# Attention and mixture of experts on one core: loads, casts and bindings moved around the change of phase

## The chip, the cores and the metric

The kernel runs on one core of a Trainium2 chip. The core has five engines with an instruction queue each: TensorE (PE in the profile, its weight loads PEld), VectorE (DVE), ScalarE (ACT), GpSimd (POOL) and SyncE (SP). SyncE computes nothing; it issues most of the DMAs. An engine takes its instructions in the order in which they were built, and one that waits holds up all that stand behind it. The metric is the device time of one execution in microseconds (us); lower is better.

## The reference

```python
def _attn_ref(q, k, v):                    # 8 batches, 8 heads, 576 positions, 64 wide
    ...
    out_d = sm_attn(q_d, k_d, v_d)         # on means of four positions
    out_up = np.repeat(out_d, factor, axis=2)
    ...
    scores = np.where(mask, scores, -1000000000.0)   # mask: |i - j| < 4
    ...
    return out_up + out_local

def _moe_ref(x, modality_id, w_gate, modality_bias, w1, w2):   # x: 4608 tokens, 512 wide
    logits = x @ w_gate + modality_bias[modality_id]
    e_idx = np.argmax(logits, axis=1)
    ...
    for e in range(E):                     # 8 experts, 512 -> 1024 -> 512
        mask = e_idx == e
        ...
        h = np.maximum(x[mask] @ w1[e], 0.0)
        out[mask] = gate_w[mask, None] * (h @ w2[e])
```

Attention over all batches gives the tokens; each token is then sent to one expert of eight.

## The kernel before

**Attention** runs in 32 stages of two heads (number n; batch b has n = 4b to 4b+3). The work of a stage is cut into steps, and the table PHASE gives each step a place after its stage's start, in stages. build() makes a list of calls (place, function), sorts it, and so writes the order of all engines by hand (tc.manual_schedule). A step of stage n with phase p has the place n + p. Steps that matter here: tp (transposes of q and k), sc and scd (scores; scd needs qd, which GpSimd sums from qe), le, exp, z, zr (softmax; z and zr on VectorE), nl (GpSimd scales the local weights with zr; on the profile's L426, tile le), nd (the same for tile de, L430), lt and Pw (turned weights), vp and vd (sums of v over four positions: a matmul on tile vw, L279, and its copy on VectorE, L284), avl (local output, L481), X (the sum of both, L488).

**Loads.** load_v(b, part) loads half of a batch's v into tile vw in four to seven DMAs (L266, L267). Two buffers vw take turns, so v of batch 7 overwrites that of batch 5. load_qk loads q and k of four heads (L244). store() writes finished tokens to the DRAM tensor xs (L634). SyncE has eight DMAs in flight at most: each waits, besides its own conditions, for the landing of the one eight ahead of it.

**Routing.** After each batch the router finds the expert and place of every token and GpSimd scatters token numbers and gates into the DRAM table tab (L640). The **early units** are two units of 512 tokens of one expert, taken from the first four batches, so that their work can begin where attention ends. moe.entries reads a unit's part of tab into a tile tg (L892). rows(u, h) then has GpSimd gather 128 of its tokens from xs into xg by those numbers (L935); the first gather of the first unit is placed at 28.64, just ahead of qe of stage 28. wload loads a 128x1024 block of the expert's first layer (tile raw, four DMAs, L849), wsplit casts it to a high part (GpSimd for the first four, L874) and takes the low part (VectorE, L880). Each product of the experts is three matmuls: high by high, high by low, low by high.

**Experts.** After the two early units (Moe.compute, first layer L1003, second layer Moe.second, L1057) come three large units of 1024 tokens (class Large), then small ones of 256, one of 128 (compute_half, H = 1, second to last) and one of 256. While early unit 1 computes, the first large unit is prepared by Large.put: "1W", "2W" cast its weights, "r0" to "r7" turn its rows, "S1", "T1" and the like are sums. In this part no order is written by hand, a scheduler sets it, and `tc.issue_after(ins)` binds what is traced inside it behind `ins` on that engine.

Of the kernel before, what the change touches and what calls it, by code (L numbers as in the profile page):

```python
# [11 lines left out]
AF = mybir.ActivationFunctionType  # L12
# [7 lines left out]
B, H, S, D = 8, 8, 576, 64  # L20
# [56 lines left out]
def whole(pieces):  # L77

    while True:
        try:  # L80
            next(pieces)
        except StopIteration as x:
            return x.value
# [720 lines left out]
class Moe:  # L804
# [180 lines left out]
    def compute(s, T, W, X, H=2, step=None, mid=None, J=None, last=0):  # L985
        nc = s.nc
        xh, xl = X
        hh, hl = s.hidden(H)
        N = 128 * H
        n = 4 // H  # L990
        early = H == 4 and s.turn["h"] == 0
        ps = {}
        for f, ks in [(f + j, k) for f in range(0, 8, 2) for k in ((0, 1), (2, 3)) for j in range(2)] if early else [
                (f, range(4)) for f in range(8)]:
            if step and f % 2 == 0 and 0 in ks:
                step()
            if f % n == 0 and 0 in ks:
                ps[f // n] = s.ps.tile([128, n, N], F32, name="l1", tag="S", bufs=SB)
            p, fs = ps[f // n], slice(128 * f, 128 * f + 128)
            for k in ks:  # L1000
                wh, wl = W[k]
                for i, (a, x) in enumerate(((wh, xh), (wh, xl), (wl, xh))):
                    nc.tensor.matmul(p[:, f % n, :], a[:, fs], x[:, k, :N], start=(k == 0 and i == 0),  # L1003
                                     stop=(k == 3 and i == 2))
            if f % n == n - 1 and 3 in ks:
                g = slice((f + 1 - n) % 4, f % 4 + 1)
                y, z = hh[f // 4][:, g, :N], hl[f // 4][:, g, :N]
                nc.scalar.activation(y, p, AF.Relu)  # L1008
                s.low = nc.vector.scalar_tensor_tensor(z, p, 0.0, y.bitcast(F32), op0=ALU.max, op1=ALU.subtract)  # L1009
        s.second(T, W[4:], hh, hl, H, step, mid, J, last)  # L1010

# [25 lines left out]
    def second(s, T, W, hh, hl, H, step, mid, J=None, last=0, large=False):  # L1037

        nc = s.nc
        if last:  # L1040
            with s.tc.issue_after(getattr(s.sent, "ins", s.sent)):
                nc.gpsimd.drain()  # L1042
        for h in range(H):
            if mid:
                mid(h)
            a, b, hs = (hh[h // 4], hl[h // 4], h % 4) if large else (hh, hl, h)
            hs = slice(128 * hs, 128 * hs + 128)

            first = large or s.turn["h"] == 0
            p = s.ps.tile([128, DM], F32, name="l2", tag="S" if first else "A", bufs=SB if first else 2)  # L1050
            for f in range(8):
                if step and f % (2 * H) == 0:
                    step()
                wh, wl = W[f // 2]
                y, z = a[f // 4][:, f % 4, hs], b[f // 4][:, f % 4, hs]
                for i, (l, x) in enumerate(((y, wh), (z, wh), (y, wl))):
                    nc.tensor.matmul(p, l, x[:, f % 2, :], start=(f == 0 and i == 0), stop=(f == 7 and i == 2))  # L1057
            o = s.xp.tile([128, DM], F32, name="o", bufs=3)
            nc.scalar.mul(o, p, T[:, h, 1:2].bitcast(F32))  # L1059
            if J is not None and not last and h < J.shape[1]:  # L1060
                o2 = s.out.rearrange("n (c d) -> (n c) d", c=2)
                for c in range(2):
                    s.sent = nc.gpsimd.indirect_dma_start(  # L1063
                        out=o2, out_offset=bass.IndirectOffsetOnAxis(ap=J[:, h, c : c + 1], axis=0),
                        in_=o[:, 256 * c : 256 * c + 256], in_offset=None, bounds_check=2 * NTOK - 1, oob_is_err=False)
                continue
            nc.gpsimd.indirect_dma_start(  # L1067
                out=s.out[:, :],
                out_offset=bass.IndirectOffsetOnAxis(ap=T[:, h, 0:1], axis=0),
                in_=o, in_offset=None, bounds_check=NTOK - 1, oob_is_err=False)  # L1070
# [123 lines left out]


def build(tc, q, k, v, mid, w_gate, bias, w1, w2, out):
    nc = tc.nc
    with ExitStack() as ctx:
# [6 lines left out]
        start = ExitStack()  # L1205
        start.enter_context(tc.manual_schedule())
        C = Consts(tc, cp, ps)
        moe = Moe(tc, ctx, C, ps, xs, tab, w1, w2, out)
        with ExitStack() as actx:
# [10 lines left out]
            C.clear(nc, cp)  # L1220
            at.load_v(0, 0)
            C.load(tc, cp, work, at.wk, mid, bias, w_gate)
            at.load_v(0, 4)
            at.load_qk(1, 0)
            start.close()
            ro.rp, ro.block = at.wk, moe.block
            N = 4 * B
# [15 lines left out]
            def call(at, f, *args):  # L1243
                calls.append((at, len(calls), f, args))

            P = PHASE
            parts = {"kT": "kT_", "Pw": "Pw_", "W": "store"}
# [5 lines left out]
            for nm, p in P.items():  # L1253
                f, i = (nm[:-1], int(nm[-1])) if nm[-1].isdigit() and nm not in ("ch1", "ch2") else (nm, 0)
# [6 lines left out]
            for b in range(B):  # L1261
                if b + 1 < B:
                    for j in range(2):
                        late_ = (1.39, 0.78)[j] if b == B - 2 else 0
                        call(4 * b - 1 + used + 0.3 + 0.8 * j - late_, at.load_v, b + 1, 4 * j)
            for h in range(3, N // 2):
                call(2 * h - 5 + last + 0.25, at.load_qk, h // 2, h % 2)
# [35 lines left out]
            def split(u):  # L1303
                piece(("x", u), lambda: moe.xsplit(E[u][2], 4), E[u].append)
# [21 lines left out]
            for u in range(KEARLY):  # L1326
                call(t + 1 + 0.1 * u, expert, u)
            for u in range(KEARLY):
                call(4 * (B - 2) + 1.3 + 0.01 * u, entries, u)
            for i, x in enumerate((0.64, 1.64, 2.64, 2.66)):  # L1330
                call(4 * (B - 1) + x, rows, 0, i)
            free = N - 1 + max(P["scd"], P["sc0"], P["sc1"]) + 0.02

            for c, x in enumerate((0.2, 2.4, 3.4, 4.4)):
                call(4 * (B - 2) + x, wload, c)
            for c in range(2):
                for j in range(2):
                    call(N - 1 + (0.15, 0.66)[c] + 0.25 * j, wsplit, c)
            calls.sort(key=lambda x: x[:2])
            with tc.manual_schedule():  # L1340
                for x in calls:
# [52 lines left out]
        lists, Es, Ts, Rs, Xs, parts = {}, {}, {}, {}, {}, {}  # L1394

        N, written = len(order), ExitStack()
# [3 lines left out]
        def gather(i):  # L1400
            nm, u, H = order[i]
            idx, ei = lists[nm]
            Es[i] = moe.expert(ei, u)
            if H == 8:
                x = Xs[i] = Large(moe, Es[i], u)
                if not u:
                    x.put("l0 l1")
                Ts[i] = x.T = moe.entries(idx, u, H)
                if u:
                    Rs[i] = [moe.unit_rows() for _ in range(2)]  # L1410
                else:
                    Rs[i] = [moe.gather(Ts[i][:, 4 * l : 4 * l + 4], H=4) for l in range(2)]
                x.R = Rs[i]
                return
            Ts[i] = moe.entries(idx, u, H)
            if i in cols:
                Js[i] = moe.columns(Ts[i], cols[i][0], cols[i][1])
            Rs[i] = moe.gather(Ts[i], H=H, J=Js.get(i))
# [37 lines left out]
        first = ("1W", "2W", "S1", "", "l2")  # L1456
        begin = ("r0 r1 r2 r3 5W S2", "r4 r5 r6 r7 1X 2X 6W", "T1 5X T2", "6X s4 t4")
# [4 lines left out]
        for i, (_, u, H) in enumerate(order):  # L1462
# [12 lines left out]
            if i < KEARLY:  # L1475
                turn = [0]

                def early_step():
                    if i == 1:
                        Xs[2].put(first[turn[0]] if turn[0] < len(first) else "")  # L1480
                    elif 0 < turn[0] < 6:
                        b, t = ((B - 2, 0), (B - 2, 1), (B - 1, 0), (B - 1, 1), (B - 1, 2))[turn[0] - 1]
                        with tc.issue_after(moe.low.ins):
                            for j in range(2):
                                ro.R(b, 2 * t + j)
                        ro.store(b, t)
                    turn[0] += 1

                def mid(h):
                    if i == 0:  # L1490
                        split(1, h)
                        if h == 3:
                            gather(2)
                    else:
                        Xs[2].put(begin[h])
                        if h == 1:
                            Js[3] = moe.pieces(lists["q"][0], 1)
                        elif h == 2:
                            moe.numbers(Js[3])

                moe.compute(Ts[i], Ws[i], Xs[i], H, early_step, mid)
            elif H == 8:
                q, count = Xs[i], iter(range(32))
# [62 lines left out]
        with tc.For_i(0, nu, 1) as iv:  # L1566
# [6 lines left out]
            Xs = whole(moe.xsplit(R))  # L1573
# [32 lines left out]
```

## Time and profile before

| what | value |
|---|---|
| time, median of 3 runs | 655.95 us (651.89 to 656.73) |
| the profiled execution's own time | 658.49 us |
| its span, first to last instruction | 656.4 us |
| PE busy / matmul instructions | 628.5 us / 6099 |
| DVE, ACT, POOL busy | 438.6, 383.9, 338.5 us |
| mean granted clock of TensorE | 0.988 |

The trace has two parts: attention up to about 242 us, then the experts. The profiled execution is one execution; it lies 2.5 us above the median of the others, and 2.1 us of its time lie outside the span.

### The profile page before, as it was taken

The page shows a single profiled execution, that of the slowest core. Times are in us where ns is not written, and L with a number is a line of the kernel's source. Part 1 is how long each engine was busy: PE and PEld are TensorE (multiplying, and loading weights), DVE is VectorE, ACT ScalarE, POOL GpSimd, SP SyncE. Part 2 cuts the span into 40 slices and gives each one's busy share as a digit, 9 for nine tenths or more (in the row PEclk, how much of TensorE's full clock was granted, in tenths as well). Part 3 has the DMA queues.
Part 4 walks back from the last instruction along what each step waited for, and adds up shares of the span by engine and source line. Part 5 has one row for each costly group of instructions (what it writes and reads, how often), then busy time and mean ns, then how long its engine had stood idle before and what let it go on. Part 6 is the DMA issues. An engine that isn't in the chain of part 4 may idle for free. (4 is left out here: it accounts for less than half of the span.)

```text
span 656.4 us, 16392 instructions
## 1 busy us (share of the span) xinstructions
PE 628.5 (96%) x6099; PEld 496.8 (76%) x6099; DVE 438.6 (67%) x896; ACT 383.9 (58%) x870; POOL 338.5 (52%) x378
## 2 busy tenths in 40 slices
PE   9899999999999789999999999999999999999995
PEld 5677677766777567887888788887888878889794
DVE  6689898899988865843455764777638875246610
ACT  4689999988999862312544732447324474245610
POOL 6644564745557761326069775688755720141211
PEclk9899999998999989999999999999999999999999
DMA  8899699999899975499012445134531345459300
GB/s 190 178 189 187 112 201 186 172 201 160 173 169 151 187 200 144 78 176 234 1 49 97 108 118 144 49 97 109 124 137 49 96 117 158 144 152 285 130 15 32
DMA packets 168860, 90.21 MB, mean 137 GB/s; under 512 B 131812, under 2 KB 153354, under 8 KB 168778
## 3 DMA queue, kind: packets, MB, share of 16 engines
q1 hardware_dynamic: 160810, 69.96, 51.2%
q0 software_dynamic: 7968, 19.18, 9.4%
q8 instruction: 49, 0.80, 0.6%
q14 instruction: 33, 0.27, 0.2%
HBM read 69.86 MB, written 19.51 MB: 136 GB/s over the span
## 5 line engine op out<-in xcount | busy, mean ns | idle before, releaser
L1057 PE MATMUL l<-V,H 128*128 128x512 f32 x792 | 183.7, 390 | 0.0
L1057 PEld LDWEIGHTS l<-V,H 128*128 128x128 f32 x792 | 148.0, 188 | 30.6
L943 POOL DMA_INDIRECT xg<-xs,m x64 | 74.4, 1163 | 19.2 <-issue 19.2
L426 POOL TENSOR_TENSOR le<-le,zr 128x384 f32<-128x384 f32 x32 | 26.6, 832 | 81.3 <-DVE zr L422 40.7
L1067 POOL DMA_INDIRECT out_dram<-o,tq x24 | 27.9, 1161 | 76.3 <-ACT o L1059 58.5
L442 ACT COPY Pw<-lt 32x288 f32<-32x288 f32 x128 | 54.6, 427 | 1.7
L1003 PE MATMUL l<-X,H 128*128 128x512 f32 (+1 forms) x240 | 53.9, 374 | 1.5 <-ACT X L979 1.0
L1059 ACT ACTIVATE o<-l,tq 128x512 f32<-128x512 f32 x24 | 16.6, 690 | 66.2 <-PE l L1057 41.4
L640 POOL DMA_INDIRECT tab<-ig,si x36 | 36.4, 1010 | 29.8 <-DVE mni L662 21.8
L1003 PEld LDWEIGHTS l<-X,H 128*128 128x128 f32 x240 | 41.5, 189 | 9.9 <-ACT X L979 1.3
L1160 ACT ACTIVATE H<-o 128x512 fp32r<-128x512 f32 x36 | 22.8, 634 | 39.2 <-DVE o L1182 39.2
L331 ACT COPY kT<-tp 64x512 f32<-64x512 f32 x64 | 37.2, 580 | 8.8 <-PE tp L294 7.3
L481 PEld LDWEIGHTS avl<-Pw,vw 128*64 128x64 f32 x768 | 33.6, 139 | 11.1 <-ACT kT L329 4.9
L880 DVE TENSOR_TENSOR V<-raw,V 128x1024 fp32r<-128x1024 f32 x22 | 35.1, 1621 | 9.9 <-ACT V L874 9.7
L481 PE MATMUL avl<-Pw,vw 128*64 128x96 f32 x768 | 39.7, 254 | 2.1 <-ACT Pw L442 2.1
L1009 DVE SCALAR_TENSOR_TENSOR H<-l,H 128x512 fp32r<-128x512 f32 x24 | 16.2, 687 | 34.5 <-ACT H L1008 34.4
L1067 POOL DMA_INDIRECT out_dram<-o,tg x10 | 11.3, 1129 | 51.6 <-ACT o L1059 35.5
L412 ACT ACTIVATE de<-scd,dm 128x144 f32<-128x144 f32 x96 | 35.2, 374 | 1.7 <-DVE dm L404 0.6
L373 PE MATMUL sc<-kT,qT 128*24 128x64 f32 x1536 | 34.8, 225 | 0.3 <-ACT qT L318 0.3
L1008 ACT ACTIVATE H<-l 128x512 fp32r<-128x512 f32 x24 | 13.9, 596 | 35.7 <-PE l L1003 35.7
L373 PEld LDWEIGHTS sc<-kT,qT 128*24 128x24 f32 x1536 | 24.6, 104 | 13.2 <-issue 10.8
L1121 DVE TENSOR_TENSOR G<-X,G 128x1024 fp32r<-128x1024 f32 x15 | 23.2, 1551 | 13.8 <-ACT G L1120 13.8
(282 smaller groups left out, 1435.5 us busy)
## 6 DMA issues: line engine op xcount, KB each, us to landing
raw<-in_moe_w_dram SPq DMA_DIRECT2D x112, 128.0 KB
raw<-in_moe_w_dram SPq DMA_DIRECT2D x28, 512.0 KB
vw<-in_v_dram SPq DMA_DIRECT2D x60, 180.0 KB
qt<-in_q_dram SPq DMA_DIRECT2D x26, 288.0 KB
kt<-in_k_dram SPq DMA_DIRECT2D x26, 288.0 KB
xs<-R SPq DMA_DIRECT2D x48, 128.0 KB
xs<-G SPq DMA_DIRECT2D x16, 128.0 KB
qt<-in_q_dram SPq DMA_DIRECT2D x6, 256.0 KB
```

The source lines that it names most:

```text
L331: s.nc.scalar.copy(s.kB[r, g, a, PAD + 64 * g : PAD + 64 * g + 512], p[r])
L373: s.nc.tensor.matmul(p[32 * j : 32 * j + SUB, 2 * i : 2 * i + 2, :], qT[:, q0 : q0 + SUB], kB[:, :, q0 : q0 + WIN], start=False, stop=(i = ...
L412: s.nc.scalar.activation(x, s.t["scd", n][:, c].rearrange("p (k x) -> p k x", k=NB), AF.Exp, bias=m[:, c : c + 1], accum_out=s.t["z", n][: ...
L426: s.nc.gpsimd.tensor_tensor(e, e, z[:, : 2 * NB].unsqueeze(2).broadcast_to([128, 2 * NB, WIN]), op=ALU.mult)
L442: s.nc.scalar.copy(s.Pw[n % NPW][r, :, j, :SUB], s.t["lt", n][r, :, :SUB])
L481: s.nc.tensor.matmul(p[64 * a : 64 * a + 64, c], vw[:, NB * (4 * (hp // 2) + hp % 2 + 2 * a) + k, :], Pw[:, 2 * k + a], start=True, stop=T ...
L640: i = nc.gpsimd.indirect_dma_start(out=s.tab[:, :], out_offset=bass.IndirectOffsetOnAxis(ap=C.si[:, t : t + 1], axis=0), in_=C.ig[:, t, :] ...
L880: (nc.gpsimd if turn == 4 else nc.vector).tensor_tensor(lo, raw, hi.bitcast(F32), op=ALU.subtract)
L943: s.nc.gpsimd.indirect_dma_start(out=R[l].rearrange("p h (i x) -> p (h i) x", i=4)[:, i, :], out_offset=None, in_=s.xs.rearrange("n (a x) ...
L1003: nc.tensor.matmul(p[:, f % n, :], a[:, fs], x[:, k, :N], start=(k == 0 and i == 0), stop=(k == 3 and i == 2))
L1057: nc.tensor.matmul(p, l, x[:, f % 2, :], start=(f == 0 and i == 0), stop=(f == 7 and i == 2))
L1067: nc.gpsimd.indirect_dma_start(out=s.out[:, :], out_offset=bass.IndirectOffsetOnAxis(ap=T[:, h, 0:1], axis=0), in_=o, in_offset=None, boun ...
```

## The change

Six things are changed. (1) Both halves of the last v (load_v for batch 7) get earlier places: 24.65 instead of 25.45 and 26.58 instead of 26.86. (2) The reading of the early units' entries goes from 25.30 to 26.62. (3) The first two weight blocks are loaded at 26.64 and 26.90 instead of 24.2 and 26.4, and their casts stand at 31.70 and 31.95 instead of 31.15 and 31.66. (4) The first puts of the large unit (1W, 2W, S1, l2) are bound behind the last ReLU of the early unit's first layer that has been traced. (5) The puts in its second layer are bound behind the last matmul of the first layer. (6) In the second layer of the unit with H = 1, four hidden blocks at a time take both products with the high part first and then the one with the low part.

```diff
-                    nc.tensor.matmul(p[:, f % n, :], a[:, fs], x[:, k, :N], start=(k == 0 and i == 0),
-                                     stop=(k == 3 and i == 2))
+                    s.mm = nc.tensor.matmul(p[:, f % n, :], a[:, fs], x[:, k, :N], start=(k == 0 and i == 0),
+                                            stop=(k == 3 and i == 2))
...
-                nc.scalar.activation(y, p, AF.Relu)
+                s.relu = nc.scalar.activation(y, p, AF.Relu)
...
-            for f in range(8):
-                if step and f % (2 * H) == 0:
+            for f, parts in [(f + j, x) for f in range(0, 8, 4) for x in ((0, 2), (1,)) for j in range(4)] if H == 1 else [
+                    (f, (0, 1, 2)) for f in range(8)]:
+                if step and f % (2 * H) == 0 and 0 in parts:
                     step()
                 wh, wl = W[f // 2]
                 y, z = a[f // 4][:, f % 4, hs], b[f // 4][:, f % 4, hs]
-                for i, (l, x) in enumerate(((y, wh), (z, wh), (y, wl))):
-                    nc.tensor.matmul(p, l, x[:, f % 2, :], start=(f == 0 and i == 0), stop=(f == 7 and i == 2))
+                for i in parts:
+                    l, x = ((y, wh), (z, wh), (y, wl))[i]
+                    nc.tensor.matmul(p, l, x[:, f % 2, :], start=(f == 0 and i == 0), stop=(f == 7 and i == (1 if H == 1 else 2)))
...
-                        late_ = (1.39, 0.78)[j] if b == B - 2 else 0
+                        late_ = (2.19, 1.06)[j] if b == B - 2 else 0
                         call(4 * b - 1 + used + 0.3 + 0.8 * j - late_, at.load_v, b + 1, 4 * j)
...
-                call(4 * (B - 2) + 1.3 + 0.01 * u, entries, u)
+                call(4 * (B - 2) + 2.62 + 0.01 * u, entries, u)
...
-            for c, x in enumerate((0.2, 2.4, 3.4, 4.4)):
+            for c, x in enumerate((2.64, 2.9, 3.4, 4.4)):
                 call(4 * (B - 2) + x, wload, c)
             for c in range(2):
                 for j in range(2):
-                    call(N - 1 + (0.15, 0.66)[c] + 0.25 * j, wsplit, c)
+                    call(N - 1 + (0.7, 0.95)[c] + 0.25 * j, wsplit, c)
...
                     if i == 1:
-                        Xs[2].put(first[turn[0]] if turn[0] < len(first) else "")
+                        with tc.issue_after(moe.relu.ins):
+                            Xs[2].put(first[turn[0]] if turn[0] < len(first) else "")
...
-                        Xs[2].put(begin[h])
+                        with tc.issue_after(moe.mm.ins):
+                            Xs[2].put(begin[h])
```

On SyncE before, around stage 25: the last block DMA of the first weights, the entries of both early units (tiles tg; ebi and eb hold their addresses), the last q and k, and the first half of the last v.

```order
L849 DMA raw_3700<-in_moe_w_dram 32x1024
L888 TENSOR_LOAD ebi
L888 ISA x2
L892 ISA
L892 DMA tg_3862<-tab 128x4x2
L888 TENSOR_LOAD eb_3338
L888 ISA x2
L892 ISA
L892 DMA tg_3874<-tab 128x4x2
L244 DMA qt<-in_q_dram 128x9x64 x2
L244 DMA kt<-in_k_dram 128x9x64 x2
L267 DMA vw_155<-in_v_dram 30x24x64 x4
```

The same place in the changed kernel; the first half of v (vw_155, x4) and qt x2 stand right ahead of these rows, and the first weights right behind the second tg.

```order
L244 DMA kt<-in_k_dram 128x9x64 x2
L267 DMA vw_155<-in_v_dram 30x24x64
L266 DMA vw_155<-in_v_dram 30x64
L267 DMA vw_155<-in_v_dram 30x23x64
L266 DMA vw_155<-in_v_dram 30x64
L267 DMA vw_155<-in_v_dram 30x23x64
L266 DMA vw_155<-in_v_dram 27x64
L267 DMA vw_155<-in_v_dram 30x23x64
L888 TENSOR_LOAD ebi
L888 ISA x2
L892 ISA
L892 DMA tg_4059<-tab 128x4x2
```

The entries stood behind four DMAs of weights; now fifteen DMAs of v, q and k stand between the same store of tokens and them.

On GpSimd before, from the last gather of the first early unit on: the two casts of weights (H_4733, H_4807), nl and nd (le, de), qe and qd of the last stage.

```order
L935 DMA xg<-xs,tg_3862 128x512
L874 CAST H_4733<-raw_3700 128x1024
L426 TENSOR_TENSOR le<-le,zr 128x384
L430 TENSOR_TENSOR de_168<-de_168,zr 128x18x24
L351 TENSOR_TENSOR qe<-qT 128x288
L355 TENSOR_TENSOR qd<-qe 128x144
L874 CAST H_4807<-raw_3700 128x1024
L1239 COPY X<-X 128x4x64
L426 TENSOR_TENSOR le<-le,zr 128x384
```

The same place in the changed kernel (the casts are H_4809 and H_4834).

```order
L935 DMA xg<-xs,tg_4059 128x512
L426 TENSOR_TENSOR le<-le,zr 128x384
L430 TENSOR_TENSOR de_168<-de_168,zr 128x18x24
L351 TENSOR_TENSOR qe<-qT 128x288
L355 TENSOR_TENSOR qd<-qe 128x144
L1241 COPY X<-X 128x4x64
L874 CAST H_4809<-raw_4072 128x1024
L874 CAST H_4834<-raw_4072 128x1024
L426 TENSOR_TENSOR le<-le,zr 128x384
```

Both casts now stand together, behind qd of the last stage and ahead of nl of stage 30. The gathers themselves keep their places on GpSimd.

On VectorE in the changed kernel, the low parts of the same two blocks (H_4809, H_4834) among the last stages' softmax steps; before, the first stood between lm and le of stage 30 and the second between its z and its zr.

```order
L416 TENSOR_REDUCE z<-le 128x4x3
L880 TENSOR_TENSOR H_4809<-raw_4072,H_4809 128x1024
L421 TENSOR_SCALAR zr<-z 128x15
L422 RECIPROCAL zr<-zr 128x15
L880 TENSOR_TENSOR H_4834<-raw_4072,H_4834 128x1024
L380 TENSOR_REDUCE lm<-sc 128x12
L437 STREAM_TRANSPOSE lt<-le 128x384
L404 TENSOR_REDUCE dm<-scd 128x3
L284 COPY vd<-vp 96x512
L488 TENSOR_TENSOR X<-avl,Od 128x288 x2
L385 TENSOR_TENSOR le<-sc,lm 128x384
L416 TENSOR_REDUCE z<-le 128x4x3
```

The low parts moved from the middle of stage 30's softmax to between its z and stage 31's lm.

## Rows read from the trace of the kernel before

**Rows 1.** Busy time of each engine by stretch: PE, PEld, DVE, ACT, POOL, clock, DMA share, GB/s

```profile
200.00:250.00 50.00, 42.03 (x657) 30.79 (x653) 35.45 (x73) 36.29 (x103) 37.69 (x40) 0.93 0.91 200
...
204.00:225.50 21.50, 18.64 (x389) 14.00 (x387) 17.20 (x39) 18.26 (x54) 20.00 (x24) 1.00 0.97 167
...
230.00:235.00 5.00, 5.00 (x52) 3.62 (x47) 2.44 (x6) 1.11 (x6) 0.00 (x0) 0.50 0.96 228
```

**Rows 2.** Timeline of PE, end of attention: start, us, line, tiles, [idle before <-releaser]

```profile
206.18 0.95 PE L399 MATMUL scd<-kd,qd 64*64 64x144 f32 x12 [0.65 <-POOL qd L355]
...
215.67 1.06 PE L279 MATMUL vp<-vw,pool 128*32 128x256 f32 x12 [1.42 <-DMA vw<-in_v_dram]
...
229.47 1.93 PE L279 MATMUL vp<-vw,pool 128*32 128x256 f32 x12 [2.40 <-DMA vw<-in_v_dram]
...
241.79 0.97 PE L1003 MATMUL l<-X,H 128*128 128x512 f32 x3 [0.99 <-ACT X L979]
```

**Rows 3.** Timeline of SyncE's DMA issues; us is issuing time, not landing

```profile
142.49 2.56 SPq L267 DMA_DIRECT2D vw<-in_v_dram  x4
...
153.77 4.83 SPq L267 DMA_DIRECT2D vw<-in_v_dram  x4
...
172.26 3.72 SPq L267 DMA_DIRECT2D vw<-in_v_dram  x4
...
184.35 4.40 SPq L267 DMA_DIRECT2D vw<-in_v_dram  x4
...
193.46 1.89 SPq L849 DMA_DIRECT2D raw<-in_moe_w_dram  x4
196.23 1.59 SPq L892 DMA_DIRECT2D tg<-tab  x2
...
201.82 5.91 SPq L267 DMA_DIRECT2D vw<-in_v_dram  x4
...
217.63 0.35 SPq L266 DMA_DIRECT2D vw<-in_v_dram  x1
...
293.61 0.40 SPq L892 DMA_DIRECT2D tq<-tab  x1
```

**Rows 4.** Timeline of POOL

```profile
203.87 1.05 POOL L935 DMA_INDIRECT xg<-xs,tg  x1 [0.30 <-issue]
...
205.70 0.43 POOL L355 TENSOR_TENSOR qd<-qe 128x144 f32<-128x144 f32 x1
...
219.21 1.04 POOL L874 CAST H<-raw 128x1024 fp32r<-128x1024 f32 x1
...
224.95 0.40 POOL L1239 COPY X<-X 128x256 f32<-128x256 f32 x1
227.27 0.83 POOL L426 TENSOR_TENSOR le<-le,zr 128x384 f32<-128x384 f32 x1 [1.92 <-DVE zr L422]
...
235.19 0.83 POOL L426 TENSOR_TENSOR le<-le,zr 128x384 f32<-128x384 f32 x1 [6.21 <-ACT PdT L459]
...
298.58 1.21 POOL L935 DMA_INDIRECT xg<-xs,tq  x1 [0.96 <-DMA tq<-tab]
```

**Rows 5.** Timeline of DVE, end of attention

```profile
221.45 1.55 DVE L880 TENSOR_TENSOR H<-raw,H 128x1024 fp32r<-128x1024 f32 x1
...
225.56 1.21 DVE L880 TENSOR_TENSOR H<-raw,H 128x1024 fp32r<-128x1024 f32 x1
...
227.04 0.49 DVE L380 TENSOR_REDUCE lm<-sc 128x12 f32<-128x384 f32 x1
...
234.79 0.25 DVE L422 RECIPROCAL zr<-zr 128x15 f32<-128x15 f32 x1
```

**Rows 6.** Timeline of PE among the experts

```profile
299.31 3.02 PE L1003 MATMUL l<-X,H 128*128 128x512 f32 x12 [0.55 <-ACT o L1059]
303.39 0.44 PE L963 MATMUL xt<-ident,xg 128*128 128x128 f32 x2 [1.07 <-DMA xg<-xs,tq]
...
621.50 0.66 PE L963 MATMUL xt<-ident,xg 128*128 128x128 f32 x4 [0.87 <-DVE H L1032]
```

## Prediction, made before the changed kernel was run

> **What bounds the kernel now.** I read the busy times by stretch first. TensorE is busy nearly throughout; its largest idle share lies between 200 and 250 us, where it works 42.03 of 50 us [rows 1]. So I read that stretch engine by engine. TensorE's timeline shows what it waits for: vp of stage 28 waits 1.42 us and vp of stage 30 waits 2.40 us, both for the last v; the first product of the early unit starts at 241.79 [rows 2]. After the second wait the granted clock is at half level, 0.50 in 230 to 235, that is 1.2 instead of 2.4 GHz, and the same vp takes 1.93 us instead of 1.06 [rows 1, 2]. These waits are what the change goes after. But GpSimd is the fuller engine just before: 20.00 of 21.5 us between 204 and 225.5 [rows 1]. It works there without a real pause from the first gather of the early unit (203.87) to the copy of X (225.35). Its idle times come after: 1.92 us before nl of stage 30 and 6.21 us before nl of stage 31 at 235.19 [rows 4]. The reader is to see in SyncE's timeline that the last v is issued late because weights, entries, q and k are issued ahead of it [rows 3]: first half from 201.82 on.
>
> Then I looked for what else stops TensorE. Among the experts three waits touch the changed code: 0.55 us behind ScalarE's output scaling, 1.07 us for the large unit's rows, 0.87 us for a PSUM buffer in the H = 1 unit [rows 6].
>
> **Part 1, v ahead of the entries.** The gain on v is plain: both halves are issued far ahead of their use, the 1.42 and the 2.40 us fall away. The cost is at the entries. In the new order SyncE issues at 193.46, where the first weights stood, first v (4 DMAs), q and k (4), v (7, three of them small), and only then the entries. The same row of four v, four q and k, four v has run twice before: from 142.49 to 153.77 + 4.83 = 158.60, that is 16.1 us, and from 172.26 to 184.35 + 4.40 = 188.75, that is 16.5 us [rows 3]. So the twelve large ones end at 193.46 + 16.3 = 209.8. Three small ones at 0.35 add 1.0, and from the last weight DMA to the entries' issue it takes 196.23 - 195.35 = 0.9 [rows 3]. The entries are then issued at 211.7. How long they take to land no row shows alone. The nearest is the table read issued at 293.61, whose reader on GpSimd starts at 298.58 after a wait ended by it [rows 3, 4]: 5.0 us at most, and more than nothing. I take the middle, 2.5, and get 214.2. From this I take 1 us, an estimate, because in both earlier rows GpSimd issued scatters beside SyncE and now it would stand still: 213.2.
>
> [...] No row here shows the landing of a lone small DMA.
>
> The first gather needs the entries, and it keeps its place on GpSimd, at 203.87 in the trace. **GpSimd would stand from 203.87 to 213.2: 9.3 us.** Behind it on GpSimd are qe and qd of stage 28; scd waits for that qd already now (0.65 us at 206.18) [rows 2], and TensorE's avd, avl and all later stages queue behind scd. So TensorE stops with it. The bounds: entries landing with no delay at 211.7 and 3 us less for quieter queues give 4.8 us; 5.0 us of landing gives 12.8 us.
>
> **Part 2, what the end of attention gives back.** Before, from the first gather to nl of stage 31: 235.19 - 203.87 = 31.3 us. In the new order the two casts leave the full stretch, so the copy of X ends 225.35 - 203.87 - 2 x 1.04 = 19.4 us after the first gather [rows 4]. Then comes a new chain. Cast one ends at 20.4; VectorE takes its low part (1.38, mean of 1.55 and 1.21 [rows 5]) to 21.8, zr of stage 30 (0.4) to 22.2, the second low part to 23.6; then ten instructions from lm to zr of stage 31, which before stood from 227.04 to 234.79 with waits and add to 4.8 without [rows 5], and 0.5 for the exp between them: 28.9 us. Gain: 31.3 - 28.9 = **2.4 us**. All of the removed v waits, 3.8, and the slow clock do not come back, since GpSimd and then the casts are late next. The bounds: nothing, if the half clock comes behind the new stall instead; 8.1 us, if the two idle times of GpSimd (1.92 + 6.21) are eaten whole.
>
> Loading the first weights later costs nothing: issued right behind the entries at about 213, they are cast 19.4 us after 213.2. That is the cover; if it goes, GpSimd waits with nl of stage 30 behind it.
>
> **Part 3, the bindings.** ScalarE now takes the cast of 2W behind two ReLUs instead of ahead of the output scaling, so the 0.55 us goes; the turnings of the first rows now stand behind all of early unit 1's first layer, so the 1.07 us goes, and second-layer products of unit 1 fill the place [rows 6]. Late next there is nothing within reach: TensorE works on. Gain 1.6, between 0 and 1.6 (the large unit's own first product comes only after both early units). On SyncE the store of the last tokens moves behind one address read and four weight DMAs of 0.3 us of issuing each; the table read at 293.61 comes later than both anyway. Nothing.
>
> **Part 4, the H = 1 unit.** Eight products with the high part now stand ahead of the second turning, so its wait of 0.87 us for VectorE's low part [rows 6] is covered by 8 x 0.23 us of matmul. No wait is on TensorE between there and its end. Gain 0.9, between 0 and 1.2.
>
> **Sum.** 9.3 - 2.4 - 1.6 - 0.9 = +4.4 us, on the profiled execution 658.49 + 4.4 = 662.9 us. The median of the runs is 655.95, 2.5 below that execution; on its scale the forecast is **660.3 us**. With each part's bounds it lies between 655.95 + 4.8 - 8.1 - 2.8 = 649.9 and 655.95 + 12.8 = 668.8.
>
> **The rivals.**
> Entries in time. If SyncE gets through fifteen DMAs by 203, or GpSimd comes late to its first gather, there is no stall. For it: twelve DMAs issue in some 8 us when nothing queues (2.56 us for four v at 142.49). Against it: both whole rows took 16 us. Then -2.4 - 2.5 = -4.9: 651.0 us; with all of the v waits given back, 3.8 instead of 2.4, 649.6.
>
> The stall eats idle time. GpSimd has 8.1 us of idle time behind it; if the late stages tighten so that all of it goes, the sum is 9.3 - 8.1 - 2.5 = -1.3: 654.7 us. For it: the engines behind GpSimd will have caught up while it stood. Against it: the new chain over the two casts.
>
> Slower, by the clock. TensorE idle for 10 us falls to half clock, as it did around its 2.40 us wait; the stage behind then becomes TensorE's. Price: 5.00 us of work in 230 to 235 at 0.50 would be 2.7 at full speed by the ratio 1.06 to 1.93, so 2.3 us. With the stall at its upper bound: 12.8 + 2.3 - 2.4 - 2.5 = +10.2: 666.1 us. It decides from an entries' landing past about 215.4 (stall over 11.5) without the clock's price, or 213.1 with it.
> The Trainium skill, page "TensorE: Matmul & The Clock Gate", Part 1, states that an idle array is put back to 1.2 GHz and that sustained work releases it; the trace agrees, with 0.50 behind the 2.40 us wait.
>
> **How the numbers follow.** One per cent, 6.6 us, is about what a measurement of this kernel can tell from no change. Chances: forecast 0.45, slower by the clock 0.20, idle time eaten 0.22, entries in time 0.13. The range runs from 651 (the rival without a stall) to 667. Faster by over 1% (below 649.4) is only the outer part of the rival without a stall and the lower bound of the sum: 0.08. Slower by over 1% (above 662.5) is most of the clock's rival and the upper part of the forecast: 0.25. The rest, 0.67, is within 1%.
>
> **What would show it.** In the changed kernel's trace vp has no wait for v. GpSimd's first gather of xg is preceded by some 9 us of idle time ended by the DMA tg<-tab, scd of stage 28 waits as long for qd, and the clock is half for a stretch behind it. The first product of the early unit starts near 249 us. The waits of 0.55, 1.07 and 0.87 us are gone. I am wrong if the first gather starts before 208, if nl of stage 31 follows it by under 27 or over 31 us, or if a new wait appears among the experts, where I let TensorE run on.

## The result, and the profile after

| | before | changed |
|---|---|---|
| median of 6 runs each | 656.17 us (651.89 to 657.82) | 663.50 us (661.17 to 665.04) |
| profiled execution, its span | 658.49, 656.4 us | 662.53, 660.8 us |
| mean granted clock | 0.988 | 0.986 |

The changed kernel takes 1.0132 times as long, with an interval of 1.0097 to 1.0168: 7.3 us more by the medians. A second set of runs on another chip gave 1.0100 [1.0057, 1.0143]. The forecast was 660.3 us in a range of 651 to 667; as a ratio it was 660.3 / 655.95 = 1.0066. So the time lies in the range, and the forecast's middle lies below the interval. Ratios and their intervals leave disturbed runs out and medians do not, so the two can differ by some tenths of a per cent; the chips of the experiments had medians of before between 660.74 and 664.83 us, so kernels of different groups are compared by their ratios.

Busy times by stretch in the changed kernel, columns as in [rows 1]:

```profile
200.00:250.00 50.00, 33.03 (x552) 24.63 (x548) 31.39 (x66) 30.89 (x93) 30.95 (x34) 0.86 0.69 151
204.00:225.50 21.50, 10.29 (x181) 7.76 (x183) 7.98 (x19) 8.86 (x27) 11.50 (x14) 0.76 0.77 163
```

TensorE lost 9.0 us of work in the first stretch against [rows 1], and between 204 and 225.5 every engine has about half of its former work. The timeline of GpSimd says what stood:

```profile
200.75 1.01 POOL L640 DMA_INDIRECT tab<-ig,si  x1 [0.17 <-issue]
212.91 1.05 POOL L935 DMA_INDIRECT xg<-xs,tg  x1 [11.15 <-DMA tg<-tab]
...
214.74 0.42 POOL L355 TENSOR_TENSOR qd<-qe 128x144 f32<-128x144 f32 x1
...
231.34 2.02 POOL L874 CAST H<-raw 128x1024 fp32r<-128x1024 f32 x2
234.95 1.72 POOL L426 TENSOR_TENSOR le<-le,zr 128x384 f32<-128x384 f32 x1 [1.58 <-DVE zr L422]
...
242.21 0.83 POOL L426 TENSOR_TENSOR le<-le,zr 128x384 f32<-128x384 f32 x1 [4.67 <-ACT PdT L459]
```

The first gather, which followed at once before [rows 4], waits 11.15 us for the entries. SyncE's timeline shows why they are late: v, q, k and v again are issued from 191.94 on, and the entries 17.6 us after that.

```profile
191.94 3.04 SPq L267 DMA_DIRECT2D vw<-in_v_dram  x4
195.08 2.90 SPq L244 DMA_DIRECT2D qt<-in_q_dram  x2
198.02 3.79 SPq L244 DMA_DIRECT2D kt<-in_k_dram  x2
201.90 2.49 SPq L267 DMA_DIRECT2D vw<-in_v_dram  x1
...
209.52 1.60 SPq L892 DMA_DIRECT2D tg<-tab  x2
```

TensorE's timeline of the same stretch:

```profile
215.22 1.70 PE L399 MATMUL scd<-kd,qd 64*64 64x144 f32 x12 [11.49 <-POOL qd L355]
...
224.12 1.04 PE L279 MATMUL vp<-vw,pool 128*32 128x256 f32 x12
...
235.11 1.06 PE L279 MATMUL vp<-vw,pool 128*32 128x256 f32 x12
...
241.91 0.66 PE L963 MATMUL xt<-ident,xg 128*128 128x128 f32 x4 [2.83 <-ACT PdT L459]
...
244.01 2.13 PE L481 MATMUL avl<-Pw,vw 128*64 128x96 f32 x24 [0.29 <-ACT Pw L442]
...
249.43 0.96 PE L1003 MATMUL l<-X,H 128*128 128x512 f32 x3 [0.99 <-ACT X L979]
```

Against [rows 2], vp's waits of 1.42 and 2.40 us are gone, and scd's 0.65 has become 11.49. At 244.01 avl takes 2.13 us instead of 1.21. And a new wait of 2.83 us stands at xt (the turning of gathered rows, L963), for PdT (ScalarE's copy of the turned de, L459, out of the same PSUM buffers, tag "T" in the code). ScalarE has PdT behind le of stage 31, whose input VectorE makes only at 239.02: behind both low parts, which stood at 221.45 and 225.56 in [rows 5], and by the new order behind lt, dm, vd and X. VectorE's timeline, and then ScalarE's row of the waits between 195 and 255 us:

```profile
232.99 1.45 DVE L880 TENSOR_TENSOR H<-raw,H 128x1024 fp32r<-128x1024 f32 x1
...
234.75 1.23 DVE L880 TENSOR_TENSOR H<-raw,H 128x1024 fp32r<-128x1024 f32 x1
...
239.02 0.54 DVE L385 TENSOR_TENSOR le<-sc,lm 128x384 f32<-128x384 f32 x1
```
```profile
ACT le L390 <- DVE le L385: 4.3, 2, 4.1
```

Among the experts the three waits of [rows 6] are gone. These are TensorE's waits there, all that the view lists from 255 us to the end (us in total, times, longest):

```profile
PE l L1059 <- ACT H L1031: 0.3, 1, 0.3
PE ht L1030 <- ACT o L1027: 0.3, 1, 0.3
```

**Where the time went.** The two spans are cut at the first gather and at the first product of the early unit. Without a wait the gather would have started 0.30 us behind the scatter that ends at 201.76, at 202.06. Before, this point was reached at 203.87, so this execution ran 1.8 us ahead by then, for no reason that the change gives. Then: the stall, 212.91 - 202.06 = +10.85; from the gather to the first product, 36.52 against 37.92 = -1.4; from the first product to the end of the span, 411.4 against 414.6 = -3.2. That makes +6.25 like for like, beside +7.3 by the medians; less the lead of 1.8 it is the 4.4 by which the spans differ.

### The profile page after: what moved, and what is told of

Its sections match the earlier page's. It is cut to its first block, busy times and chain, and to the rows that moved or that the text cites. A ratio compares the mean times of both kernels' runs of the same rounds, so it can differ in the third digit from the quotient of the medians.

```text
span 660.8 us, 16389 instructions
## 1 busy us (share of the span) xinstructions
PE 626.7 (95%) x6099; PEld 496.9 (75%) x6099; DVE 440.9 (67%) x896; ACT 383.5 (58%) x870; POOL 340.3 (51%) x378
## 5 line engine op out<-in xcount | busy, mean ns | idle before, releaser
L1069 POOL DMA_INDIRECT out_dram<-o,tq x24 | 28.9, 1203 | 76.3 <-ACT o L1061 58.9
L640 POOL DMA_INDIRECT tab<-ig,si x36 | 36.5, 1013 | 24.5 <-DVE gt L581 14.7
L399 PE MATMUL scd<-kd,qd 64*64 64x144 f32 x384 | 31.4, 297 | 11.5 <-POOL qd L355 11.5
L1008 ACT ACTIVATE H<-l 128x512 fp32r<-128x512 f32 x24 | 14.2, 596 | 36.4 <-PE l L1003 36.3
```

What stands on the lines that cost most here:

```text
L399: s.nc.tensor.matmul(p[r, c, :], qd[r, 40 * c : 40 * c + 64], kd[r, :], start=True, stop=True, skip_group_check=True)
L640: i = nc.gpsimd.indirect_dma_start(out=s.tab[:, :], out_offset=bass.IndirectOffsetOnAxis(ap=C.si[:, t : t + 1], axis=0), in_=C.ig[:, t, :] ...
L1069: nc.gpsimd.indirect_dma_start(out=s.out[:, :], out_offset=bass.IndirectOffsetOnAxis(ap=T[:, h, 0:1], axis=0), in_=o, in_offset=None, boun ...
```

## The experiments

The theory was that the wait for the entries is the whole loss; the rivals lay in the casts' place and in the order of v, q and k.

**1. Entries back.**

```diff
-                call(4 * (B - 2) + 2.62 + 0.01 * u, entries, u)
+                call(4 * (B - 2) + 1.3 + 0.01 * u, entries, u)
```

> The changed kernel with the entries' place alone put back (25.30). They then stand behind the first half of the last v (four DMAs) only, and v stays early. Theory (the whole loss is GpSimd's wait for the entries, 11.15 us in the changed kernel's trace): the wait falls under 2 us, scd's wait for qd with it, the first product of the early unit starts near 240, and the time is 651 us (649 to 654), below both kernels. Rival (the loss is in the casts and low parts that now stand together among the last two stages): these are unchanged, so the time stays at 660 or above.

Measured: 1.0021 [0.9978, 1.0063]; median 665.50 beside 663.62 us. The stall is gone, and yet the kernel is not faster than before. TensorE's timeline, and GpSimd's last nl:

```profile
207.05 0.95 PE L399 MATMUL scd<-kd,qd 64*64 64x144 f32 x12 [1.37 <-POOL qd L355]
...
217.17 1.08 PE L298 MATMUL tp<-ident,kt 128*128 128x128 f32 x4 [6.45 <-DMA kt<-in_k_dram]
...
241.37 1.12 PE L963 MATMUL xt<-ident,xg 128*128 128x128 f32 x4 [2.83 <-ACT PdT L459]
...
249.14 0.96 PE L1003 MATMUL l<-X,H 128*128 128x512 f32 x3 [0.99 <-ACT X L979]
```
```profile
204.75 1.05 POOL L935 DMA_INDIRECT xg<-xs,tg  x1 [1.12 <-ACT PdT L459]
...
241.67 0.83 POOL L426 TENSOR_TENSOR le<-le,zr 128x384 f32<-128x384 f32 x1 [5.12 <-ACT PdT L459]
```

From the gather to the first product it now takes 249.14 - 204.75 = 44.4 us instead of 36.5. So the theory in its strong form fell: 0.8 to 1.1% hangs on the entries (1.0021 against the changed kernel's 1.0100 and 1.0132), but behind the stall other late things had been hidden: TensorE now waits 6.45 us for kt, and the 2.83 us at xt stayed.

**2. Entries late alone**, in the kernel before (the edit above the other way round).

> The kernel before with only the entries' place moved, to 26.62: they stand behind the first eight weight DMAs, q, k and the first half of v. Theory: GpSimd's first gather waits 10 us or more, and the time is 664 to 668 us. Rival (casts and low parts carry the loss): they stand as before, so the time is 656 to 658, the stall being paid for by idle time of GpSimd behind it.

Measured: 1.0196 [1.0141, 1.0252], median 676.79 beside 663.62 us. The theory's 664 to 668 us were 1.012 to 1.018 times the 655.95 of before; the ratio lies just above, and its interval reaches into them. The gather's wait, with the first two blocks of weights in front too:

```profile
217.58 1.05 POOL L935 DMA_INDIRECT xg<-xs,tg  x1 [12.64 <-DMA tg<-tab]
```

The late entries alone make the kernel slower; the rest of the change does not need to be there. So the stall's cost is shown from both sides: added here, taken away in experiment 1.

**3. The bindings and the H = 1 order alone** (in the kernel before, these pieces of the diff and no place).

> The kernel before with only the two bindings of the large unit's puts and the new order of products in the H = 1 unit; attention and all loads as before. Theory: the waits of 0.55, 1.07 and 0.87 us are gone and nothing takes their place, 2.5 us less: 653.7 us (652.5 to 655). Rival (TensorE's wait only moves, or weight and gather queues set the same end): 656 us, and a new wait of 0.5 us or more stands among the experts.

Measured: 0.9896 [0.9851, 0.9941], an interval that rests on three of its six runs; by the medians of all, 660.45 to 663.62, it is 0.995. The waits of 0.55, 1.07 and 0.87 us are gone and none took their place; the view of TensorE's waits from 255 us on lists the same two of 0.3 us as in the changed kernel. The trace is the finer measure: from the first product of the early unit to the end of the span it takes 414.6 us before; in the eleven traces of kernels that have the bindings 411.4 to 413.6, mean 412.5; without them 414.7 in experiment 2 and 418.3 in experiment 5. That last trace has 2.0 us of idle time near 478 us for which the view names no releaser; experiments 6 and 7 have 1.7 and 0.7 us of it at the same place. Without experiment 5 the gain is 2.1 us.

**4. Gathers behind qe and qd.**

```diff
-            for i, x in enumerate((0.64, 1.64, 2.64, 2.66)):
+            for i, x in enumerate((1.66, 2.2, 2.64, 2.66)):
```

> The changed kernel with the first two gathers of the early unit moved on GpSimd from 28.64 and 29.64 to 29.66 and 30.20, which puts them behind qe and qd of stages 28 and 29; the entries stay late. Theory (what costs is not the late entries but what stands behind the waiting gather): scd of stage 28 no longer waits for qd, GpSimd's wait at the first gather shrinks to 2 to 4 us, and the time is 653 to 656 us. Rival (late entries make the early unit's rows late, wherever the gather stands): TensorE waits at the turnings xt of the early unit for xg, and the time stays at 660 or above.

Measured: 1.0078 [1.0039, 1.0118]. The time is the rival's (660 us and more, 1.006 times 655.95), the mechanism is neither's. In the profiled execution SyncE reached the first v at 203.54 and the entries at 221.74, so the gather, though later, waited no less:

```profile
226.10 1.04 POOL L935 DMA_INDIRECT xg<-xs,tg  x1 [13.06 <-DMA tg<-tab]
```

No turning of the early unit waited for its rows, which the rival wanted. scd did not wait for qd, but tp waited 6.60 us for kt, as in experiment 1, and pdt (the turning of what nd scales, L451) 2.40 and 2.09 us for GpSimd's nd:

```profile
220.55 1.08 PE L298 MATMUL tp<-ident,kt 128*128 128x128 f32 x4 [6.60 <-DMA kt<-in_k_dram]
...
230.23 0.28 PE L451 MATMUL pdt<-ident,de 64*96 64x64 f32 x1 [2.40 <-POOL de L430]
```

**5. v early alone**, in the kernel before (only `late_` of the diff).

> The kernel before with only both halves of the last v moved to their early places; the first weights stay ahead of all. The first half then stands ahead of the entries and of the last q and k. Theory (SyncE's queue is full there, so whatever goes ahead makes the next one late): TensorE's turnings tp wait 5 us or more for kt, GpSimd's first gather waits for the entries, and the time is 1.006 to 1.012 times that of before. Rival (early v gives back TensorE's 1.42 and 2.40 us, and q and k have room): 0.994 to 0.997.

Measured: 1.0058 [1.0015, 1.0100], medians 662.29 to 660.74. Just slower, at the theory's lower bound of 1.006, but not by its mechanism: no wait for kt and none for v is in the profile, and the first product starts at 241.22, as before (241.79).

```profile
204.58 1.05 POOL L935 DMA_INDIRECT xg<-xs,tg  x1 [0.30 <-issue]
```
```profile
241.22 0.96 PE L1003 MATMUL l<-X,H 128*128 128x512 f32 x3 [0.99 <-ACT X L979]
```

Removing vp's 3.8 us of waits moved the first product by 0.6, or by 1.3 counted from the first gather (36.6 against 37.9 us); in experiment 3, with v as before, that stretch took 36.4. The profile shows nothing that would make the kernel slower but the idle time near 478 us, which experiments 6 and 7 have too; so that it is slower rests on the runs alone, and why is open.

**6 and 7. q and k first, with the casts back and with the casts late.** The changed kernel with entries at 25.30 and

```diff
-                        late_ = (2.19, 1.06)[j] if b == B - 2 else 0
+                        late_ = (1.39, 1.06)[j] if b == B - 2 else 0
...
-                    call(N - 1 + (0.7, 0.95)[c] + 0.25 * j, wsplit, c)
+                    call(N - 1 + (0.15, 0.66)[c] + 0.25 * j, wsplit, c)
```

where the seventh leaves the second piece out.

> The changed kernel with three things put back: entries at 25.30, the first half of v at 25.45 (so behind q and k), both casts at 31.15 and 31.66. Left of the change: the first weights behind v, the second half of v at 26.58, the bindings and the H = 1 order. Theory (the loss is in the order entries, q and k, v, and in the casts' place; late weights cost nothing): no wait of over 1 us for kt, vw or the entries; the time is 0.990 to 0.996 times that of before. Rival (the weights land too late for the casts at their old places): GpSimd waits over 1 us at a cast for raw, and the ratio is 0.998 or above.

> The same kernel as the one with q and k first, but with the two casts and low parts at the places of the changed kernel (31.70 and 31.95). Theory (with casts and low parts together, VectorE's le of stage 31 comes late and TensorE stops 2.83 us at the turning xt): 3 to 5 us above that kernel, a ratio of 0.996 to 1.003. Rival (moving the casts is neutral or a gain, since GpSimd has idle time at both places): within 1 us of it.

Measured: 0.9973 [0.9930, 1.0015] and 1.0017 [0.9976, 1.0059], medians 659.57 and 662.53 us. By the ratios the late casts cost 0.44%, 2.9 us, the lower end of what was expected and hardly beyond the noise: the two intervals overlap. GpSimd's casts in the one and in the other:

```profile
221.49 1.05 POOL L874 CAST H<-raw 128x1024 fp32r<-128x1024 f32 x1
...
228.80 1.04 POOL L874 CAST H<-raw 128x1024 fp32r<-128x1024 f32 x1 [2.21 <-DMA raw<-in_moe_w_dram]
```
```profile
229.77 1.04 POOL L874 CAST H<-raw 128x1024 fp32r<-128x1024 f32 x1 [2.95 <-DMA raw<-in_moe_w_dram]
...
234.10 1.04 POOL L874 CAST H<-raw 128x1024 fp32r<-128x1024 f32 x1 [3.29 <-DMA raw<-in_moe_w_dram]
```

Both wait for the late weights, so the rival of the sixth run is partly borne out. SyncE's order is the same in both, yet it issued the entries at 193.69 in the one and at 200.32 in the other, and the five DMAs from vw on took 6.52 and 10.00 us to issue. So the longer waits of the seventh can't be laid to the casts' place alone. In its trace kt is 1.72 us late though q and k go first:

```profile
214.25 0.63 PE L298 MATMUL tp<-ident,kt 128*128 128x128 f32 x4 [1.72 <-DMA kt<-in_k_dram]
...
250.51 0.96 PE L1003 MATMUL l<-X,H 128*128 128x512 f32 x3 [0.99 <-ACT X L979]
```

From the gather (205.44) to the first product it takes 45.1 us, as long as the 44.4 of experiment 1. So most of kt's wait went and the time stayed: the kt wait alone is not what keeps experiment 1 from being faster.

**8. Casts back, entries late** (the changed kernel with only the second piece above).

> The changed kernel with only the two casts put back to 31.15 and 31.66; entries and v as changed. Theory (the casts' place adds to the stall): GpSimd waits 11 us at the first gather as in the changed kernel, the 2.83 us wait at xt goes, and the ratio to before is 1.004 to 1.009 instead of 1.013. Rival (behind the stall everything is late anyway, the casts only fill another hole): 1.012 to 1.015.

Measured: 1.0132 [1.0066, 1.0199], the changed kernel's own ratio: the rival held. The xt wait is gone, but with a stall of 13.28 us it buys nothing that the runs show.

```profile
219.97 1.05 POOL L935 DMA_INDIRECT xg<-xs,tg  x1 [13.28 <-DMA tg<-tab]
```

**9. q and k first, entries late** (only the first piece above), on one chip with the changed kernel itself.

> The changed kernel as it is, once more, on the chip of the three beside it. 1.010 to 1.016 times the kernel before, with GpSimd waiting 10 to 14 us at the first gather.

> The changed kernel with only the first half of the last v put back to 25.45, behind q and k; the entries stay late and have the same fifteen transfers ahead of them. Theory (two waits lie beside each other: GpSimd's for the entries and TensorE's 6.5 us for kt, and the longer one counts): the stall is unchanged at 10 to 13 us, and the time is that of the changed kernel within 2 us. Rival (the two waits add, kt being late behind the stall as well): 3 to 6 us below the changed kernel.

Measured: 1.0100 [1.0057, 1.0143] and 1.0144 [1.0077, 1.0211], medians 672.00 and 673.49. The gather's wait in the two:

```profile
222.30 1.04 POOL L935 DMA_INDIRECT xg<-xs,tg  x1 [12.64 <-DMA tg<-tab]
```
```profile
220.60 1.05 POOL L935 DMA_INDIRECT xg<-xs,tg  x1 [10.83 <-DMA tg<-tab]
```

Putting q and k first brings nothing while the stall stands, so the rival, 3 to 6 us below the changed kernel, is out. The theory's "within 2 us" is within the noise: 1.5 us apart by the medians, 2.9 by the ratios. In neither trace does TensorE wait for kt behind the stall.

**10. Entries and casts back, v early** (the edits of experiments 1 and 8).

> The changed kernel with entries and casts put back, v early in both halves, ahead of q and k. Theory (v ahead of q and k makes kt late, and with the stall gone this wait is on the path; the casts cost nothing at their old place): TensorE waits 3 to 7 us for kt, 2 to 5 us above the kernel with q and k first and the casts back (0.9973), so 1.000 to 1.005. Rival (kt's wait is covered by idle time behind it): 0.996 to 0.999.

Measured: 0.9942 [0.9895, 0.9989], median 661.52 beside 664.83 of before and 672.00 of the changed kernel on the same chip. Better than either expectation, and the one version beside experiment 3 that the runs put below both kernels. The trace does have the waits that the theory feared, 2.70 us for kt and, at the cast, 5.97 us for the late weights:

```profile
216.03 0.63 PE L298 MATMUL tp<-ident,kt 128*128 128x128 f32 x4 [2.70 <-DMA kt<-in_k_dram]
```
```profile
228.22 1.03 POOL L874 CAST H<-raw 128x1024 fp32r<-128x1024 f32 x1 [5.97 <-DMA raw<-in_moe_w_dram]
```

Its first product starts at 247.03, 40.8 us behind the gather, and 2.2 us of the gain over before are the bindings' shorter second part; what the other runs gained that this profile did not is open. The 0.9942 is no better than the bindings and the H = 1 order alone (0.9896, experiment 3): no run shows a gain from the moved loads.

**11. A version meant to beat both**: experiment 3 and the second half of v ahead of the second block of weights.

```diff
-                        late_ = (1.39, 0.78)[j] if b == B - 2 else 0
+                        late_ = (1.39, 1.30)[j] if b == B - 2 else 0
```

> A version meant to beat both: the kernel before with the two bindings and the H = 1 order, and of the loads only the second half of the last v moved, ahead of the second block of first weights (26.34 instead of 26.86; those weights stay at 26.4). Theory (the second v's wait of 2.40 us goes, and nothing that is needed sooner comes later): 2.5 us from the bindings and 0 to 2.4 from v, 0.992 to 0.997. Rival (the block of weights comes too late for its cast at 31.66, and GpSimd waits there for raw): 0.998 or more.

Measured: 1.0347 [1.0283, 1.0411]. At 26.34 the load is built ahead of avl of stage 23, whose two halves stand at 26.53 and 26.54; avl then takes batch 7's v in place of its own and waits for it (the profile puts the wait down to the weights issued right behind v, which avl doesn't read):

```profile
218.66 2.19 PE L481 MATMUL avl<-Pw,vw 128*64 128x96 f32 x24 [29.91 <-DMA raw<-in_moe_w_dram]
```

So its time says nothing about the weights. The changed kernel's 26.58 is 0.04 stages behind that avl: in this table v cannot go further ahead.

**The runs together**, as ratios to before:

| entries | casts | first half of v ahead of q, k | behind q, k |
|---|---|---|---|
| late | late | 1.0132, 1.0100 (changed) | 1.0144 |
| late | back | 1.0132 | |
| early | late | 1.0021 | 1.0017 |
| early | back | 0.9942 | 0.9973 |

The entries are worth 0.8 to 1.9%, the casts' place 0.4 to 0.8% once the entries are early and nothing while they are late, the place of v's first half nothing that these runs show.

## Why the prediction was right

The mechanism was right and the sum was too small: +4.4 us forecast, +6.25 measured like for like. The stall was 1.55 us longer and the end of attention gave back 1.0 us less; the second part gave 0.7 us more. Two close agreements are luck: the profiled execution's 662.53 us beside 662.9, and its first product at 249.43 beside "near 249". Without its lead of 1.8 us the product would stand at 251.2.

**Part 1** was right in mechanism, and 1.55 us too small: 9.3 forecast, 10.85 measured. The issuing was well judged. From the first v to the entries it took 17.6, 17.3, 17.1 and 18.2 us in the four traces with that order; the prediction had 18.2, less 1 us for quieter queues; no row gave a price for that 1 us, and in the mean of the four 0.7 came. The mis-sized term is what follows: from the issue to the gather 2.5 was taken, and it took 3.4 (212.91 - 209.52), with both reads being issued in it: 0.9 of the 1.55. In the other traces with late entries it took 2.9 to 4.4. Of the rest, 0.4 is the issuing (17.6 for 17.2) and 0.3 that GpSimd had run 1.8 us ahead by then and SyncE only 1.5 (193.46 - 191.94).

**Part 2** came out at 1.4 us back to the first product instead of 2.4, though nl of stage 31 followed the first gather by 29.3 us, close to the 28.9 forecast; the avl at 244.01 then took 0.9 us more, with the granted clock at 0.75 between 240 and 245, behind the 2.83 us wait at xt, which the prediction did not have. The sentence that v's waits "do not come back" held in experiment 5. That late weights cost nothing held only under its cover, as the prediction said: with the stall removed GpSimd's single waits for them are 0.81 us in experiment 1 and 2.21 to 5.97 us in experiments 6, 7 and 10.

**Parts 3 and 4** were right: all three waits are gone, none took their place, 3.2 us in this profile and 2.1 in the mean of all against 2.5.

**The rivals.** "Entries in time" did not happen in any of the five kernels in which the entries stand behind v, q and k. Its time of 651 us for a kernel without the stall, 0.9925 times before, would have been wrong too: experiment 1 took the stall away and stayed at 1.0021. The casts' place is part of the reason (with the casts back as well, 0.9942 in experiment 10); how the rest divides between kt and the weights no run separates.

"The stall eats idle time" hardly came: GpSimd's two idle times were 1.58 and 4.67 us instead of 1.92 and 6.21, so 1.9 of the 8.1 us were eaten.

"Slower by the clock" is the nearer one by the time, and not by its mechanism. The 663.5 us lie 3.2 above the forecast and 2.6 below its 666.1, and its ratio of 1.0155 lies within the interval. The change is slower by over 1%, to which the prediction gave a chance of 0.25. On the scale of before the entries came at 212.91 + 1.8 = 214.7, past its point of 213.1 with the clock's price and short of 215.4 without. The clock was 0.76 between 204 and 225.5, and scd took 1.70 us instead of 0.95. But the stage behind the stall did not become TensorE's: GpSimd worked from the gather at 212.91 to the end of both casts at 233.36 without a wait of over 0.2 us, and reached that end 20.45 us after the gather, where the prediction had 21.5. What the half clock cost later, between 240 and 245, no run takes apart.

None of the three marks of a wrong prediction came: the gather started behind 208, nl followed it by 29.3 us, and no new wait stands among the experts.

## What to carry to other kernels

Where one queue is full of large loads (fifteen took 16.7 to 18.2 us to issue here), a load that is moved ahead makes everything it passes late. So count who waits for each thing passed, and put a tiny table read whose reader stands in front of a busy engine's queue ahead of the large loads. A stall hides other late things: the sum of waits removed is no forecast, and an experiment that removes one wait must be read for the next one. Compare pieces by cutting the trace at common instructions: the second part came out 1.0 to 3.2 us shorter in each of the eleven traces with the bindings, while the medians of the kernel before lay up to 8.7 us apart from one set of runs to the next.

## What the runs showed of the hardware

Fifteen transfers of v, q and k took 16.7 to 18.2 us to be issued in five traces on several chips, steadily, while the point at which SyncE reached them varied from 191.94 to 203.54 us. What paces them is seen in the traces: SyncE's 390 DMAs use eight semaphores in turn, and each of its waits for a landing of its own DMAs (19 before, 12 in the changed kernel) ends with the one eight ahead. In some executions TensorE already waited before that: 2.79 us for v at 192.60 in the second profile of the changed kernel. Why some executions come there so much later no run here tells apart.
